# A two-layer decode kernel: reciprocal roots, weight loads and the turn's projection regrouped

## The chip, the cores and the metric

The kernel runs on one NeuronCore of a Trainium2 chip. Its engines are TensorE (PE; its weight loads are shown apart as PEld), VectorE (DVE), ScalarE (ACT), GpSimd (POOL) and SyncE (SP, which issues the DMAs). The metric is device time of one execution in microseconds (us), the median of several runs.

## What is computed

Eight sequences (B = 8) of one token each go twice through an attention layer over a cache and an MLP, with the same weights and the same cache both times. All tensors are bf16.

```python
def _A_ref(x, k_cache, v_cache, wq, wo):      # x: 8 x 1 x 448; caches: 8 x 8 x 4096 x 256
    q = (x @ wq).reshape(B, Sq, 16, 256)...   # 16 query heads on 8 kv heads
    scores = einsum("bhqd,bhkd->bhqk", q, k) * 256 ** -0.5
    o = einsum("bhqk,bhkd->bhqd", softmax(scores), v)
    return o.reshape(B, Sq, 4096) @ wo
def _B_ref(x, w1, w2, w3, w4):
    ...
    x1 = x + hs                               # with one token, hs is 0 and x1 is x
    return x1 + _gelu(_layernorm(x1) @ w3) @ w4

x = x + _A_ref(_layernorm(x), ...)
x = x + _B_ref(_layernorm(x), ...)
x = x + _A_ref(_layernorm(x), ...)
x = x + _B_ref(_layernorm(x), ...)
```

In the mixer, each quarter of the hidden state is shifted by one or two tokens; with a single token only padding is left, so w1 and w2 are not read.

## The kernel before

**Data.** K and V of one kv head are 2 MB each and come in four chunks of 512 KB. SBUF holds 31 slots of one chunk each. One DMA brings one, two or four chunks (1 MB: two). A pair `m` (0 to 3) is two kv heads of one sequence; `s` (0, 1) is the head within the pair, `c` the chunk. Names in the order of the work: A3m2 is layer 0, sequence 3, pair 2; B3m2 is the same in layer 1.

**Work on a pair.** `kpart` (L836) turns each K chunk so that TensorE can multiply it by q: by 32 x 32 block transposes on DVE (L914) into another slot, or by TensorE transposes (L832) that ACT copies back (L892). Then come the scores (L902, L923, L951) and the softmax. `vpart` (L1034) multiplies the probabilities by V in one of two ways. The usual one has the probabilities stationary and V moving (L1089), eight rows of a PSUM bank that ACT and DVE evict (L1100, L1102) and eight small matmuls gather (L1111). The other one, `still`, has V stationary (L1063); each chunk c of each head s has four columns of its own in one bank of psV, and after both heads DVE adds the four chunks (L1066, `rd`) and scales by the reciprocal sum (L1069, `o`). `still` is taken for the last pair of a sequence in layer 0 (pair 3) and for the last pair of all (sequence 7, layer 1, pair 0). `outproj` (L1130) and, for all eight sequences at once in layer 1, `outproj8` (L1143) multiply a pair's output by its rows of wo, 16 matmuls for each head (L1138, L1151), into columns of psT.

**The turn.** When layer 0 of sequence b is through, `turn(b)` (L649) takes it to layer 1. It is one chain of small instructions: add the eight partial products of wo and x (L657, L659); normalise (`norm1`, L556: column sum on PE L526, L561 to L567 on DVE, a sum over the partitions on POOL L570, a reciprocal root on DVE, `root`, L530); w3 (`project`, L582, L584); gelu (L592 to L597); w4 (`down`, L607); the residual (L668); a second `norm1`; wq for one row (`rows_`, L678, 32 matmuls, in eight groups of four, two rows of psT at each of four partition offsets; row r = 0 for heads 0 to 7, r = 1 for 8 to 15); ACT scales all of it by the root (L685); four matmuls turn it into columns (L690); and the query of pairs 1, 2 and 3 is spread for the scores (`diagonal`, L616: L630 on DVE, L637 on PE, L643 on DVE). Only then can the scores of layer 1 begin.

**What is kept.** The K of pairs 1 to 3 stays in SBUF from layer 0 to layer 1. Four of pair 3's chunks wait, transposed, in PSUM banks during the turn (`staying`, L818: two banks psK; psX and one psS; one psV and the other psS), since their slots are needed. `unpark` (L1186, L1190) copies them into slots on ACT after the turn. The piece in psS that is copied first (`unpark(b, 1, ready, [1])`, L684) is ordered after the last operation of the turn's second root.

**The root.** `root` computes 1/sqrt by a bit trick (a shift and a subtraction) and a polynomial, as eight DVE operations for one column, ten where the weight differs by column. The turn needs two of them after its first `norm1` (one for each of two norms whose sums are shared) and one after the second; the start needs one, the end two.

**Order.** Every instruction is recorded by `add` with an engine, a cost, the buffers that it reads and writes, the PSUM banks and units (loads) that it touches, and a priority. A bank may be used by one engine at a time: an operation of another engine depends on all operations of the engine before it in that bank, whatever the columns. `schedule` (L168) then fixes the order on every engine once and for all, by a list schedule that takes the lowest priority number among what is ready by its own costs. The turn's operations have -1.0, except the eight groups of wq, which have `at[0] + 1.5`, behind the V matmuls around them. Engines run their list in order and wait on semaphores. SP issues all loads in one fixed order (`order`, L1248; the stream of L1216 to L1245), each after the last readers of the slots that it overwrites. At the start that order is the rows of x, the first K pair, wq in three pieces of 128 rows and two of 64 rows (`wqt0`, `wqt1`, the last 64 rows of wq folded into the two halves of the partitions), then K, V and wo; w3 (again three pieces and two of 64 rows) and w4 come just before the V of the first sequence's pair 3.

**The end.** `end` (L768) does, for all eight sequences together, what the turn does up to the residual: add the eight partial products of psT (L777) and x (L779), normalise (`norm8`, L719), w3, two roots, gelu, w4, the residual, a transpose back (L797), a copy (L802) and the output DMA (L803).

Of the kernel before, what the change touches and what calls it, by code (L numbers as in the profile page):

```python
# [3 lines left out]
P = 128  # L4
B = 8
D = 448
HQ = 16
HKV = 8
# [3 lines left out]
NCH = 4  # L12
NSLOT = 31
SMALL = 218
# [3 lines left out]
NS = 2  # L18
# [22 lines left out]
ROOT_MAGIC = 0x5F1FFFF9  # L41
ROOT_K = 0.703952253
ROOT_C = 2.38924456
# [29 lines left out]
class Unit:  # L73


    def __init__(self, name, emit, nbytes, slotted=True):
        self.name, self.emit, self.nbytes, self.slotted = name, emit, nbytes, slotted
        self.wide = None
        self.slot = self.sem = self.val = None
        self.op = None  # L80
        self.readers = []
        self.land = None
        self.evs = [None, None]
        self.raw, self.source = False, None
        self.group, self.lead, self.pair = [self], None, None
# [273 lines left out]
def bass_interleave_layers__gqa_block_cached__mixer_s_mlp__decode_kernel(  # L359
# [49 lines left out]
    sf, rcs, stat = pack(f32, [8, NP * 4, NS * 10])  # L409
# [20 lines left out]
    def rows(u, t, ap, nbytes):  # L430
# [84 lines left out]

    ROOT = -0.375 * ROOT_K ** 5
    EPS1 = LN_EPS * D ** 3
    EPS2 = LN_EPS * LN_EPS * D ** 3 / (1.0 + LN_EPS)
    SCALE1 = -ROOT * float(D) ** 0.5
    SCALE2 = -ROOT * (D / (1.0 + LN_EPS)) ** 0.5  # L520

# [8 lines left out]
    def root(out, v, second, square, bufs, units, name, scalar=False):  # L530


        c, io = 160, i32
        eps, scale = (EPS2, SCALE2) if second else (EPS1, SCALE1)

        def op(emit, n):
            dve(emit, c, bufs if n != "0" else square, bufs, units=units, name=name + n)

        def weigh(n):

            if scalar:
                op(lambda e: e.scalar_tensor_tensor(v(2), out(), v(1), out(), ALU.mult, ALU.mult), n)
            else:
                op(lambda e: e.tensor_tensor(v(2), out(), out(), ALU.mult), n)
                op(lambda e: e.tensor_tensor(v(2), v(2), v(1), ALU.mult), n + "b")

        op(lambda e: e.tensor_scalar(v(1), v(0), eps, scale ** -2.0, ALU.add, ALU.mult), "0")
        op(lambda e: e.tensor_single_scalar(out().bitcast(io), v(1).bitcast(io), 1, ALU.arith_shift_right), "1")
        op(lambda e: e.tensor_scalar(out().bitcast(io), out().bitcast(io), -1, ROOT_MAGIC, ALU.mult, ALU.add), "2")
        weigh("3")  # L550
        op(lambda e: e.scalar_tensor_tensor(out(), v(2), -ROOT_C, out(), ALU.add, ALU.mult), "4")
        weigh("5")
        op(lambda e: e.scalar_tensor_tensor(v(2), v(2), -10.0 / (3.0 * ROOT_K ** 2), v(2), ALU.add, ALU.mult), "6")
        op(lambda e: e.scalar_tensor_tensor(out(), v(2), 5.0 / ROOT_K ** 4, out(), ALU.add, ALU.mult), "7")

    def norm1(x, bx, bx4, out0, name):  # L556


        c = 160
# [7 lines left out]
        dve(lambda e: e.tensor_tensor_reduce(out=sjk[:, :], in0=sxc[:, 0:4], in1=sxc[:, 0:4], scale=1.0, scalar=0.0,  # L567
# [4 lines left out]
        root(lambda: sf[:, 2:3], lambda k: sf[:, (1, 3, 4)[k]:(2, 4, 5)[k]], name.endswith("a"), [Bs["sq"]], [Bs["f"]], [], name + "n", True)  # L572
# [41 lines left out]
    Bo1, Bo2 = [[Buf() for _ in range(HKV // 2)] for _ in range(2)], [Buf() for _ in range(HKV // 2)]  # L614
# [34 lines left out]
    def turn(b):  # L649
# [5 lines left out]
        dve(lambda e: e.memset(sx1[64:128, 4:5], 0.0), 125, [], [Bs["x4"]], name=n + "c1")  # L655
        plan.turn = True
# [735 lines left out]
```

## Time and profile before

| what | value |
|---|---|
| median of 3 runs | 1097.46 us (1096.98 to 1097.98) |
| the profiled execution | 1098.74 us |
| its span on the core | 1095.7 us |
| mean granted TensorE clock | 0.619 |
| PE, PEld busy | 756.3 us (69%), 526.6 us (48%) |
| DVE busy | 832.6 us (76%) |
| ACT, POOL busy | 207.8 us (19%), 71.4 us (7%) |
| DMA queue of SP | 446.80 MB, 98.4% of 16 engines' span |
| L914, DVE transposes of K | x544, 649.4 us busy |
| L1089, V matmuls | x1528, 181.1 us busy |

The span is what the trace shows; 3.0 us of the execution lie around it. A timeline row gives start, duration, engine, line, operation, out<-in, shapes and count, and in brackets the idle time before it and what ended it. A row of stretches gives from:to, length, busy time of each engine with its number of instructions, the granted clock, the share of the DMA engines that is busy, and GB/s. Turn 3, used in what follows, runs from about 488.8 us (last V matmul of layer 0) to 504.2 us (first score of layer 1).

### The profile page before, as it was taken

The page shows a single profiled execution, that of the slowest core. Times are in us where ns is not written, and L with a number is a line of the kernel's source. Part 1 is how long each engine was busy: PE and PEld are TensorE (multiplying, and loading weights), DVE is VectorE, ACT ScalarE, POOL GpSimd, SP SyncE. Part 2 cuts the span into 40 slices and gives each one's busy share as a digit, 9 for nine tenths or more (in the row PEclk, how much of TensorE's full clock was granted, in tenths as well). Part 3 has the DMA queues.
Part 4 walks back from the last instruction along what each step waited for, and adds up shares of the span by engine and source line. Part 5 has one row for each costly group of instructions (what it writes and reads, how often), then busy time and mean ns, then how long its engine had stood idle before and what let it go on. Part 6 is the DMA issues. An engine that isn't in the chain of part 4 may idle for free.

```text
span 1095.7 us, 33703 instructions
## 1 busy us (share of the span) xinstructions
PE 756.3 (69%) x15400; PEld 526.6 (48%) x15400; DVE 832.6 (76%) x1595; ACT 207.8 (19%) x314; POOL 71.4 (7%) x232
## 2 busy tenths in 40 slices
PE   2566586778577865867767787577666786676864
PEld 2355454465346543555436554355444654356533
DVE  4999459964997499955899469984799739995572
ACT  1032121112021211203112032121221121121210
POOL 0000000000000000000000000000100000000000
PEclk9997566556655665556655556555655566555665
DMA  9999999999999999999999999999999999999994
GB/s 353 406 419 420 395 406 426 422 412 408 429 423 415 412 425 427 421 405 409 424 426 420 411 412 429 426 417 394 427 427 423 419 399 428 427 422 411 410 427 176
DMA packets 54846, 448.94 MB, mean 410 GB/s; under 512 B 5536, under 2 KB 11568, under 8 KB 14128
## 3 DMA queue, kind: packets, MB, share of 16 engines
q1 hardware_dynamic: 54704, 446.80, 98.4%
q8 instruction: 120, 1.97, 0.7%
q14 instruction: 22, 0.18, 0.0%
HBM read 446.77 MB, written 0.01 MB: 408 GB/s over the span
## 4 chain that ended last, share of the span: by engine, by line
DVE 39%; DMA 24%; PE 21%; issue 9%; ACT 3%; POOL 0%; POOLq 0%; DVEq 0%
DVE slots L914 29%; DMA slots<-in_A_k_cache_dram 16%; DMA slots<-in_A_v_cache_dram 8%; PE psV L1089 6%; PE psS L923 5%; DVE pT L1021 2%; PE psT L678 2%; ACT slots L892 2%; PE psS L902 2%; DVE slots L1102 1%; PE psV L1063 1%; PE psT L607 1%; PE psK L832 1%; PE psT L1138 1%; DVE qe L643 1%
## 5 line engine op out<-in xcount | busy, mean ns | idle before, releaser
L914 DVE STREAM_TRANSPOSE slots<-slots 128x1024 bf16<-128x1024 bf16 x544 | 649.4, 1228 | 33.0 <-DMA slots<-in_A_k_cache_dram 24.3
L923 PE MATMUL psS<-qe,slots 128*128 128x8 bf16 x5760 | 225.3, 175 | 152.6 <-DVE slots L914 111.5
L923 PEld LDWEIGHTS psS<-qe,slots 128*128 128x128 bf16 x5760 | 191.1, 104 | 238.5 <-DVE slots L914 176.0
L1089 PE MATMUL psV<-slots,pT 128*8 128x512 bf16 x1528 | 181.1, 550 | 17.5 <-DMA slots<-in_A_v_cache_dram 9.5
L892 ACT COPY slots<-psK 128x1024 bf16<-128x1024 bf16 x80 | 78.8, 1014 | 168.0 <-PE psK L832 167.6
L832 PE MATMUL psK<-ident,slots 128*128 128x128 bf16 x640 | 74.2, 301 | 4.2 <-DMA slots<-in_A_k_cache_dram 4.1
L1100 ACT ACTIVATE slots<-psV 128x512 bf16<-128x512 f32 x48 | 29.0, 605 | 218.5 <-PE psV L1089 218.4
L985 POOL PARTITION_ALL_REDUCE small<-small x64 | 23.8, 372 | 693.5 <-DVE small L983 582.4
L832 PEld LDWEIGHTS psK<-ident,slots 128*128 128x128 bf16 x640 | 61.1, 138 | 7.0 <-DMA slots<-in_A_k_cache_dram 4.9
L1063 PE MATMUL psV<-pT,slots 128*128 128x2 bf16 x1568 | 50.9, 166 | 17.1 <-DMA slots<-in_A_v_cache_dram 15.9
L951 PE MATMUL psS<-slots,qe 128*8 128x512 bf16 x184 | 55.4, 587 | 6.7 <-DVE slots L914 5.4
L1063 PEld LDWEIGHTS psV<-pT,slots 128*128 128x128 bf16 x1568 | 47.3, 104 | 19.7 <-DMA slots<-in_A_v_cache_dram 16.1
L1089 PEld LDWEIGHTS psV<-slots,pT 128*8 128x8 bf16 x1528 | 31.5, 90 | 50.5 <-issue 20.9
L1021 DVE STREAM_TRANSPOSE pT<-psS 128x128 bf16<-128x128 bf16 x64 | 44.9, 702 | 6.5 <-PE psS L1013 4.7
L1006 ACT ACTIVATE pT<-psS 128x128 bf16<-128x128 f32 x56 | 15.5, 277 | 178.7 <-DVE psS L1003 178.6
L1066 DVE TENSOR_REDUCE small<-psV 128x8 f32<-128x32 f32 x16 | 2.8, 174 | 58.5 <-PE psV L1063 58.5
L1111 PE MATMUL psV<-same,slots 128*128 128x4 bf16 x320 | 14.0, 166 | 43.0 <-DVE slots L1102 36.9
L630 DVE TENSOR_TENSOR qe<-psT,small 128x32 bf16<-128x32 f32 x32 | 6.1, 190 | 48.2 <-PE psS L923 34.3
L902 PE MATMUL psS<-qo,slots 128*128 128x2 bf16 x768 | 27.8, 167 | 17.6 <-ACT slots L892 10.5
L1102 DVE TENSOR_TENSOR slots<-psV,slots 128x512 bf16<-128x512 f32 x48 | 32.3, 672 | 10.0 <-ACT slots L1100 10.0
L902 PEld LDWEIGHTS psS<-qo,slots 128*128 128x128 bf16 x768 | 24.0, 101 | 25.4 <-ACT slots L892 17.1
L1111 PEld LDWEIGHTS psV<-same,slots 128*128 128x128 bf16 x320 | 11.8, 102 | 49.2 <-issue 40.8
(170 smaller groups left out, 805.8 us busy)
## 6 DMA issues: line engine op xcount, KB each, us to landing
slots<-in_A_v_cache_dram SPq DMA_DIRECT2D x149, 1024.0 KB, 9.7
slots<-in_A_v_cache_dram SPq DMA_DIRECT2D x50, 2048.0 KB, 19.1
slots<-in_A_k_cache_dram SPq DMA_DIRECT2D x44, 2048.0 KB, 18.1
slots<-in_A_k_cache_dram SPq DMA_DIRECT2D x71, 1024.0 KB, 13.7
slots<-in_A_v_cache_dram SPq DMA_DIRECT2D x14, 512.0 KB, 8.1
wo_sb<-in_A_wo_dram SPq DMA_DIRECT2D x4, 896.0 KB, 19.5
wq_sb<-in_A_wq_dram SPq DMA_DIRECT2D x3, 1024.0 KB, 9.1
w_sb<-in_B_w_dram SPq DMA_DIRECT2D x1, 1568.0 KB, 16.9
```

The lines of the kernel that those rows point to most:

```text
L832: last = e.transpose(tile[:, j * P:(j + 1) * P], slots[u.slot][:, o:o + P], ident[:, :])
L892: return e.copy(slots[u.slot][:, 1024 * t:1024 * t + 1024], tile)
L902: last = e.matmul(o, slots[u.slot][:, i:i + P], q, start=(cc == 0), stop=(cc == 1))
L914: return e.transpose(o, i)
L923: last = e.matmul(o, slots[u.slot][:, i:i + P], qe[:, 128 * k + 64 * s + 8 * g:128 * k + 64 * s + 8 * g + 8], start=(g == 0), stop=(g == 7))
L951: last = e.matmul(o, q, K[:, lo:hi + 1:hi - lo, :, g, :], start=(g == 0), stop=(g == 7))
L1021: add("dve", lambda e: e.transpose(pZ[:, :, 0:3:2].rearrange("p n s r -> p n r s"), psS[x][:, 128:192].bitcast(bf).rearrange("p (n r s) -> ...
L1063: last = e.matmul(o, slots[u.slot][:, i:i + P], w, start=(j == 0), stop=(j == 7))
L1089: last = e.matmul(psV[x][32 * i:32 * i + 8, :].rearrange("p (k d) -> p k d", k=2), w, v, start=(s == 0 and c == 0), stop=(s == 1 and c == ...
L1100: add("act", lambda e: e.activation(part(0), psV[x][:, :], ACT.Copy), 590, [], [Bhalf[0]], [bV[x]], [v], prio=at - 1, name=n + "ve0").targ ...
L1102: add("dve", lambda e: e.tensor_tensor(part(1), psV[x][:, :], part(0), ALU.subtract), 590, [Bhalf[0]], [Bhalf[1]], [bV[x]], [v], prio=at - ...
L1111: last = e.matmul(to[:, 4 * cc:4 * cc + 4].rearrange("p (s h) -> p s h", s=2), part(k // 2)[:, i:i + P], w, start=(k == 0), stop=(k == 3))
```

## The change

Six edits:

1. **Root**: another bit trick (one multiplication of the bit pattern by -1/2) and other polynomials: six operations for one column, eight where the weight differs. For the turn's roots the scale and epsilon are put into the sum of squares (`scale`, `scalar` of L567), and the other norm's root takes one operation more, seven in all.
2. **`still`**: all four chunks of a head add up in PSUM (four columns for a head), with no `rd`; each head is scaled by itself as soon as its four chunks are done (`o0`, `o1`). In layer 1 the two heads have different psV banks, in layer 0 the same one.
3. **Output projection of the last pair, by head**: its 16 matmuls for head 0 are issued after `o0`, those of head 1 after `o1`. The turn and the end add up the earlier products and x beforehand (`ao`, `xa`), then the first head's product (`xb`), and at last the second one's (`x1`).
4. **Turn's wq in two halves**: heads 0 to 7 into psT as before, heads 8 to 15 into the psS bank whose parked piece is copied out first; one row each; each is scaled by ACT into its own half of a slot (`qr0`, `qr1`) and turned into columns by itself (`qc0`, `qc1`). The groups have the turn's priority, -1.0. The first copy out of psS is ordered after the third of the root's six operations (`plan.ops[-4]`).
5. **Loads**: the four 64-row pieces of wq and w3 come first of all; `wqt1` and `w3t1` are issued by ACT ahead of everything else that it does, the other two by SP ahead of x.
6. `small` is two columns wider; a root's scratch has one part more.

The order that results on PE around turn 3 (V: L1089 or L1063 in the old line numbers, W: one head's 16 matmuls of the output projection, aS and bS: the column sums L526, wq00 to wq13: the groups of L678, ve: an eviction):

```
before: A3m3 V00 V01 V02 V03 V10 V11 V12 V13, B2m2V00, W30 W31, B2m2V01, aS, w3, V02 V03, w4, V10, bS, V11,
        wq00 wq01, V12 V13, wq02 wq03 wq10 wq11 wq12 wq13, B2m3V00 V01, qc, V02, q1s, V03, scores
after:  A3m3 V00 V01 V02 V03, W30, V10 V11 V12 V13, W31, B2m2V00, aS, V01, w3, V02 V03, w4, V10, bS, V11,
        wq00 wq01 wq02 wq03, V12 V13, wq10 wq11, qc0, wq12 wq13, B2m3V00, q1s, V01, qc1, scores (V02, V03 among them)
```

and on ACT: before, eviction of B2m2, copy out of psS, `qr`; after, copy out of psS, `qr0`, eviction of B2m2, `qr1`.

The diff, cut to its core:

```diff
-ROOT_MAGIC = 0x5F1FFFF9
+ROOT_MAGIC = 0x5F3759DF - 2 ** 31
...
+    U_side = [U_wq.pop()]
...
+    U_side.append(U_w3.pop())
+    for u in U_side:
+        u.side = True
+    U_even = [U_wq.pop(), U_w3.pop()]
+    wq_rest, w3_rest = ([U_side[i], U_even[i]] for i in range(2))
...
+        if first:
+            op(lambda e: e.tensor_scalar(v(1), v(0), *first), "0", True)
+        op(lambda e: e.tensor_scalar(out().bitcast(io), v(1).bitcast(io), -0.5, ROOT_MAGIC, ALU.mult, ALU.add), "1")
+        if scalar:
+            op(lambda e: e.scalar_tensor_tensor(v(2), out(), v(1), out(), ALU.mult, ALU.mult), "2")
+        else:
+            op(lambda e: e.tensor_tensor(v(2), out(), out(), ALU.mult), "2")
+            op(lambda e: e.tensor_tensor(v(2), v(2), v(1), ALU.mult), "2b")
+        op(lambda e: e.scalar_tensor_tensor(v(3), v(2), ROOT_Q[0], v(2), ALU.add, ALU.mult), "3")
+        op(lambda e: e.scalar_tensor_tensor(v(2), v(2), ROOT_P[0], v(2), ALU.add, ALU.mult), "4")
+        op(lambda e: e.scalar_tensor_tensor(out(), v(3), ROOT_Q[1], out(), ALU.add, ALU.mult), "5")
+        op(lambda e: e.scalar_tensor_tensor(out(), v(2), ROOT_P[1], out(), ALU.add, ALU.mult), "6")
...
-        dve(lambda e: e.tensor_reduce(sjk[:, :], psT[:, 0:32].rearrange("p (s c) -> p c s", c=4), axis=AX.X, op=ALU.add),
+        dve(lambda e: e.tensor_reduce(sjk[:, :], psT[:, 0:24].rearrange("p (s c) -> p c s", c=4), axis=AX.X, op=ALU.add),
             180, [], [Bs["jk"]], [bT], name=n + "ao")
-        dve(lambda e: e.tensor_tensor(sx1[:, 0:4], sjk[:, :], x[:, 0:4], ALU.add), 150, [Bs["jk"], Bx[b]], [Bs["x1"]], name=n + "x1")
+        dve(lambda e: e.tensor_tensor(sjk[:, :], sjk[:, :], x[:, 0:4], ALU.add), 150, [Bs["jk"], Bx[b]], [Bs["jk"]], name=n + "xa")
+        outproj(*last, [0])
+        dve(lambda e: e.tensor_tensor(sjk[:, :], psT[:, 24:28], sjk[:, :], ALU.add), 150, [Bs["jk"]], [Bs["jk"]], [bT], name=n + "xb")
+        outproj(*last, [1])
+        dve(lambda e: e.tensor_tensor(sx1[:, 0:4], psT[:, 28:32], sjk[:, :], ALU.add), 150, [Bs["jk"]], [Bs["x1"]], [bT], name=n + "x1")
...
-        ready = plan.ops[-1]
+        ready = plan.ops[-4]
...
+        v, bank = kept[b, 3][1, 0], staying(b, 1)[1]
+        E = unpark(b, 1, ready, [1], -1.0)
+        Brow, B2 = [Buf(), Buf()], [(psT, bT), (psS[parts[0, b, 2].x], bank[1])]
         for r in range(2):
+            to, bb = B2[r]
...
-                        last = e.matmul(psT[32 * g:32 * g + 2, :], syn[:, 4 - r if k == 3 else k, 1 - r:3 - r], w,
-                                        start=(r == 0 and k == 0), stop=(r == 1 and k == 3))
+                        last = e.matmul(to[32 * g:32 * g + 1, :], syn[:, 4 - r if k == 3 else k, 1:2], w, start=(k == 0), stop=(k == 3))
...
+            R = add("act", lambda e, to=to, part=part: e.activation(part(), to[:, :], ACT.Copy, scale=sf[:, 2:3]), 590,
+                    [Bs["f"]], [Brow[r]], [bb], [v], name=n + f"qr{r}")
+            R.deps[E] = False
...
+        columns(0)
+        diagonals[1, b, 1] = diagonal(1, b, 1)
+        C = columns(1)
...
-            x = bank
             for s in range(2):
+                x = bank ^ s if layer else bank
...
-                            o = psV[x][:, 16 * s + 4 * c + 2 * cc:16 * s + 4 * c + 2 * cc + 2]
+                            o = psV[x][:, 4 * s + 2 * cc:4 * s + 2 * cc + 2]
...
-            add("dve", lambda e: e.tensor_reduce(red.rearrange("p (s k) -> p s k", s=2),
+                made.append(add("dve", lambda e, s=s, x=x: e.tensor_tensor(both(out_)[:, s], psV[x][:, 4 * s:4 * s + 4].rearrange("p (c j) -> p c j", c=2),
+                                                                           rc[:, s].unsqueeze(1).to_broadcast([P, 2, 2]), ALU.mult),
+                                110, [Brc[y]], [bo[s]], [bV[x]], prio=at - 1, name=f"{n}o{s}"))
...
-    order = [U_s0] + stream[:1] + U_wq + stream[1:10] + U_wo + stream[10:]
+    order = U_side[:1] + U_even[:1] + U_side[1:] + U_even[1:] + [U_s0] + stream[:1] + U_wq + stream[1:10] + U_wo + stream[10:]
...
+        if e == "act":
+            for u in U_side:
+                u.emit(eng, u).then_inc(u.sem, 16)
```

The end is changed like the turn: `eao` adds six of the eight parts, `exa` x, `exb` the first head's and `ex1` the second head's product of the last pair.

More of the change, by code (lines that the diff above doesn't have):

```diff
@@ L528, in total, with root @@
         add("pe", emit, 110, bufs + [Bwgt], [], [bT], units, name=name)
[L530 removed]
+    def root(out, v, first, square, bufs, units, name, scalar=False):
         c, io = 160, i32
[L534 to L554, printed above, removed]
@@ new lines, in turn, with columns, emit @@
+            R.deps[E] = False
+        def columns(r):
+            def emit(e):
+                for j in range(4):
+                    last = e.matmul(psT[:, 64 + 16 * r:80 + 16 * r].rearrange("p (g j) -> p j g", j=4)[:, j],
+                                    slots[v.slot][:, 512 * r + P * j:512 * r + P * j + P],
+                                    ident[:, :].rearrange("p (g r) -> p r g", g=4)[:, 0], start=True, stop=True)
+                return last
+            return add("pe", emit, 300, [Brow[r], Bc], [], [bT], [v], name=n + f"qc{r}", n=4)
@@ L1205, in V @@
             ahead.append((b, m, s, -0.5 if s == HKV // 2 - 1 else at[0] + 1.5))
-            for x in [x for x in ahead if x[0] <= turns[0]]:
+            for x in [x for x in ahead if x[0] <= turns[0] and x[2] < HKV // 2 - 1]:
                 outproj(*x)
```

115 lines of the change are left out of this document (59 added, 56 removed).

## The prediction

> **What bounds the kernel now.** I read the page's DMA rows first, then stretches of the trace around one turn, then the timelines of that turn and of the end.
>
> ```profile
> DMA  9999999999999999999999999999999999999994
> GB/s 353 406 419 420 395 406 426 422 412 408 429 423 415 412 425 427 421 405 409 424 426 420 411 412 429 426 417 394 427 427 423 419 399 428 427 422 411 410 427 176
> ...
> HBM read 446.77 MB, written 0.01 MB: 408 GB/s over the span
> ```
>
> The DMA engines are busy in every slice, at about 422 GB/s where nothing disturbs them, while DVE, the busiest compute engine, has 76%. 446.77 MB at 422 GB/s are 1058.7 us of the 1095.7. So the time is this stream, and the other 37.0 us are the start, dips of the rate and the end. An edit pays only where it fills one of these.
>
> Stretches of turn 3 (us; granted clock, DMA share, GB/s):
>
> ```profile
> 480.55:490.55 10.00, 0.50 0.99 383
> 490.55:498.55 8.00, 0.50 1.02 422
> 498.55:504.55 6.00, 0.82 0.92 345
> 504.55:514.55 10.00, 0.65 1.01 424
> ```
>
> Two dips: (422-383)/422 x 10 = 0.92 us just before the turn's chain and (422-345)/422 x 6 = 1.09 us at its end. The same cuts at all eight turns lose 0.1, 0.4, 0.6, 0.9, 0.6, 0.7, 0.4, 0.5 (4.2 us) and 0.8, 0.8, 0.5, 1.1, 0.7, 1.0, 0.9, 0.7 (6.5 us). **10.7 us is all that the turns can give**, however long their chains of small instructions are.
>
> Why the second dip? PE rows of the timeline:
>
> ```profile
> 495.55 1.65 PE L607 MATMUL psT<-qe,w_sb 128*128 128x1 bf16 x56 [0.91 <-DVE qe L597]
> 497.13 0.60 PE L1089 MATMUL psV<-slots,pT 128*8 128x512 bf16 x4
> 497.67 0.26 PE L526 MATMUL psT<-small 128*128 128x1 bf16 x4
> 497.86 0.60 PE L1089 MATMUL psV<-slots,pT 128*8 128x512 bf16 x4
> 498.47 1.02 PE L678 MATMUL psT<-wq_sb,qe 128*2 128x512 bf16 x8
> 499.28 1.07 PE L1089 MATMUL psV<-slots,pT 128*8 128x512 bf16 x8
> ```
>
> In a turn only four pairs of slots rotate; SP reissues a pair when L1089 (or L1063) has consumed it. The V pair that landed at 495.8 is consumed only at 498.46, since PE's fixed order puts it behind the MLP's down product (L607) and the column sum (L526), which waits on the chain. SP's issues stand at 491.31, 494.68, 498.50, 500.39: 3.4 and 3.8 us apart where 1 MB takes 2.48 us at 422 GB/s. Their times to landing fall from 9.3 us to 8.4 and 7.1: the queue ran dry. So the links of the turn count only as far as they release PE for the V matmuls.
>
> **The end**, from the last V piece on (PE and DVE rows):
>
> ```profile
> 1082.28 1.01 PE L1063 MATMUL psV<-pT,slots 128*128 128x2 bf16 x32 [1.63 <-DMA slots<-in_A_v_cache_dram]
> 1083.33 0.19 DVE L1066 TENSOR_REDUCE small<-psV 128x8 f32<-128x32 f32 x1 [7.14 <-PE psV L1063]
> 1083.55 0.19 DVE L1069 TENSOR_TENSOR qo<-small 128x8 bf16<-128x8 f32 x1
> ...
> 1083.80 1.02 PE L1151 MATMUL psT<-qo,wo_sb 128*128 128x8 bf16 x32 [0.51 <-DVE qo L1069]
> 1084.86 0.42 DVE L777 TENSOR_REDUCE slots<-psT 128x32 f32<-128x256 f32 x1 [1.11 <-PE psT L1151]
> 1085.31 0.19 DVE L779 TENSOR_TENSOR slots<-slots,small 128x32 bf16<-128x32 f32 x1
> ```
>
> After the last V piece nothing runs beside this chain, so each link taken out is time. The start, in stretches (busy times of PE, PEld, DVE, ACT, POOL, then clock, DMA share, GB/s):
>
> ```profile
> 2.00:4.00 2.00, 0.00 (x0) 0.00 (x0) 1.65 (x6) 0.01 (x1) 0.00 (x0) 1.00 0.80 229
> ...
> 13.00:14.00 1.00, 0.80 (x11) 0.80 (x12) 0.90 (x7) 0.00 (x0) 0.00 (x0) 1.00 0.99 193
> 14.00:15.00 1.00, 1.00 (x12) 0.93 (x9) 0.45 (x3) 0.62 (x1) 0.00 (x0) 1.00 1.07 254
> 15.00:16.00 1.00, 0.19 (x2) 0.00 (x0) 0.00 (x0) 1.00 (x2) 0.00 (x0) 1.00 1.06 238
> ```
>
> The stream ramps up until 4 us (0.47 MB moved: 2.9 us lost) and then drops to about 230 GB/s where the two 64-row pieces of wq pass; with the stretch 16 to 17 (377) that is 1.5 us lost.
>
> **The change, part by part.**
>
> *End.* The sum over the chunks moves into PSUM, so L1066 and its gap go: 1083.33 to 1083.55, 0.22. Only the second head's 16 matmuls of L1151 follow the last piece: half of 1.02, 0.51. The wide L777 is done ahead of it, and one addition of L779's price stays: 1084.86 to 1085.31, 0.45. Together 1.18. The two reciprocal roots go from 10 to 8 operations each; the 20 of before run interleaved from 1087.41 (L547) to 1089.43 (L743), 2.02 us, so 4 of them are 0.40. The up product beside them ends near 1088.0, before their new end, so it doesn't catch up. **-1.6 us** (-1.2 if a semaphore hop eats the gaps, -1.8).
>
> *Start.* wq's and w3's 64-row pieces (0.75 MB) go first, one half of each from SP, the other from ACT, whose table load (0.73, 1.28 us) moves behind two issues of some 0.4 us (SP's first: 0.39); ACT's next work is at 14.38, so that is free. The 1.5 us of the slow stretch and 0.2 us at 116 to 120 (0.11 MB of w3 tail twice at 306) vanish there; K's first load is issued two issues later (1.18 to about 2.0), and the small loads must fill the ramp. SP's first big load goes out 0.44 earlier (0.74 for 1.18). If the halves run side by side: -0.44 - 1.7 = -2.1. If they keep 230 GB/s: 0.75 MB take 3.3 us where 422 takes 1.8, so 1.5 comes back, less what the ramp hides: -0.6 to -2.1. No row of before has ACT issuing or two queues at once: I take **-1.4**, nearer to the case with the ramp, as 2.9 us of it are empty. Upper end +0.4: two issues of 0.4 ahead of K that hide nothing. The stream never waits for q here (422 from 17 on), so the shift goes through to the end.
>
> The Trainium skill, "DMA: Bandwidth & Descriptors", section "Rules for kernel authors", speaks against this part: two transfers to disjoint partition halves serialize, because both spray over the same 16 engines, and issuing from several engines saves only issue time. By that rule the halves would keep their slow rate. The rows at 13 to 16 are of one queue and can't decide.
>
> *Turns.* Chain: a head's output is scaled alone, so between the last V matmul (488.81) and x1 there remain one scaling (0.18), 16 matmuls (0.50) and one addition (0.17) with hops: x1 ends near 489.8, not 491.17. A V block (0.6) now stands ahead of the column sum L526 instead of ahead of the projection, so 1.1 of these 1.3 us are left. First roots: 13 operations where 16 took 1.7 us, -0.3. The down product then starts near 494.1 (495.55) and ends before the V pair lands at 495.8; that pair is consumed by 497.3 (498.46), with L526 still between its halves, and SP's issue comes 1.1 us earlier. What that is worth I read from the other loads of the turns, by how far an issue is ahead of the moment at which the packets of the load before it begin: at 0 (this load) the stream lost 0.4 to 0.8 us, at 0.7 to 0.95 0.3 to 0.45, at 1.0 to 1.4 0.2 to 0.4, at 1.7 0.2. So **-0.35 per turn**.
>
> Against it: (1) Both heads still share a psV bank in layer 0, and the scaling of head 0 reads it, so the first V matmul of head 1 now waits for V03, the scaling (0.18) and, in PE's order, for 16 matmuls of the output projection (0.50): with hops 0.9 us. It ran at 485.52 right behind. Behind it on PE stand only the last two V pieces, which land at 487.76, but SP's next issue (486.57) waits for it and goes out near 487.5, in the first dip: from 1.7 us ahead to 0.8, +0.25 per turn. (2) The wq products now outrank the V pair that landed at 498.1: all of the first half (16, two groups of 1.02) stand ahead, 497.3 to 499.3; the pair (1.07) is done at 500.4, as before (500.36): 0. (3) The second half waits for the parked piece of psS (ACT L1190, 1.01), now started after the third of six root operations: 498.6 to 499.6, ahead of the pair's end (500.4), so nothing behind it on PE is later: 0. Scores of the turn start near 502.7 instead of 504.16; that releases loads which lie 5 to 8 us behind the packets, so it is hidden. Net -0.1 x 8, and I take **-1.0** with rounding; ends -6.5 (the whole second dip) and +5.5 (below).
>
> **Sum**: -1.6 - 1.4 - 1.0 = **-4.0**. The profiled execution has 1098.74 (span 1095.70 and 3.04 around it), so 1094.7 for such a one; it lies 1.28 above the median of the runs, 1097.46, which gives **1093.5**.
>
> **Rivals.** *Links in full*: if the V pair's issue is early enough, the second dips (6.5 us) go: -1.6 - 1.4 - 6.5, 1088.0. For it: the chain is 1.6 to 2 us shorter; against: V11 stays behind L526. 0.12. *Half rate stays*: the 64-row pieces run at 230 GB/s from two queues as from one, and the ramp hides none of it, -0.6 for the start: 1094.3. For it, the rows at 13 to 16; against it, the empty ramp. 0.20. (This is where the skill's rule would lead.) *Only the end counts*: the stream's dips merely move and the start is filled with the same slow bytes: 1095.9, no measurable change (the runs spread over 1.0 us, and 0.2%, 2.2 us, is about what can be told). 0.14. *Slower*: head 1's V wait, (1). If scaling and projection hold it 1.7 us or more instead of 0.9, the issue falls behind the packets and the full dip of 0.84 comes, +0.7 x 8 = 5.5, against -1.6 - 1.4: 1100.0. It needs V03 late or a busy DVE; DVE is idle from 483.3 to 488.85. 0.06. The forecast keeps 0.48.
>
> Faster 0.80, same 0.14, slower 0.06. The range: down to 1089.0, where the end and the start are at their lower bounds (-0.9) and the turns give two thirds of the second dips (-4.6 for -1.0); up to 1096.5, the third rival and 0.6 for the spread of the runs. It leaves out the first and the last rival, 0.18.
>
> **What would show it.** End: from the last V matmul's end to the output's issue 9.2 us instead of 10.75. Start: no stretch under 300 GB/s at 13 to 16, full rate by 4.5. Turns: dip at the chain's end about 0.5 us instead of 0.8, the one before it larger by 0.2; V11 of the pair done 1.1 us earlier. Wrong, if the dips vanish altogether, or if the first 5 us lose more than 4.

## The result and the profile after

| | median (runs) | range | ratio to before, 95% interval |
|---|---|---|---|
| before | 1098.04 us (14) | 1096.98 to 1100.22 | |
| changed | 1096.53 us (14) | 1093.48 to 1099.53 | 0.9984 [0.9976, 0.9991] |
| changed, a second series | 1095.28 us (12) | 1093.99 to 1098.15 | 0.9975 [0.9964, 0.9986] |

The change saves 1.5 us in the first comparison and 2.8 us in the second; all its 26 runs together have a mean of 1096.13 us with a standard error of 0.31, and before has 1098.36 (0.09) over the 157 runs that were made of it. That is 2.2 us with an error of 0.3; 4.0 were forecast. Part of the distance to 1093.5 is the starting point: three runs had given a median of 1097.46 for before, later series gave 1097.9 to 1098.4.

The profiled execution has 1096.3 us, its span 1094.5. The page's row of GB/s looks like that of before:

```profile
GB/s 357 405 420 417 411 400 428 422 404 409 428 422 417 411 428 426 422 395 423 426 426 419 399 423 426 426 416 398 427 428 424 400 406 426 426 423 414 416 425 188
...
HBM read 446.77 MB, written 0.01 MB: 408 GB/s over the span
```

The stream is still the bound, so again the dips have to be looked at. The stretches of turn 3, with the cuts of before moved by the 0.4 us by which the last V matmul of layer 0 ends earlier (488.42; after the length come the busy times of PE, PEld, DVE, ACT and POOL with their instructions, then clock, DMA share, GB/s):

```profile
480.15:490.15 10.00, 7.60 (x201) 6.41 (x198) 3.09 (x15) 0.28 (x1) 1.21 (x4) 0.50 0.98 367
490.15:498.15 8.00, 7.40 (x152) 4.14 (x152) 4.34 (x33) 0.40 (x2) 0.80 (x2) 0.50 1.00 413
498.15:504.15 6.00, 4.70 (x90) 2.11 (x83) 1.97 (x8) 3.60 (x5) 0.00 (x0) 0.95 1.01 421
504.15:514.15 10.00, 9.73 (x277) 7.51 (x277) 4.47 (x12) 4.53 (x6) 0.94 (x3) 0.57 1.01 420
```

The second dip (345 GB/s before) is gone: 421. The first one is deeper, 367 for 383. That is the main reading of this case, and the chain's PE rows show why the second one went:

```profile
493.73 1.66 PE L609 MATMUL psT<-qe,w_sb 128*128 128x1 bf16 x56 [0.33 <-DVE qe L599]
495.31 0.60 PE L1115 MATMUL psV<-slots,pT 128*8 128x512 bf16 x4
495.85 0.26 PE L531 MATMUL psT<-small 128*128 128x1 bf16 x4
496.04 0.60 PE L1115 MATMUL psV<-slots,pT 128*8 128x512 bf16 x4
496.65 1.45 PE L695 MATMUL psT<-wq_sb,qe 128*1 128x512 bf16 x12
...
498.31 0.83 PE L1115 MATMUL psV<-slots,pT 128*8 128x512 bf16 x8
```

The down product starts 1.82 us earlier (493.73 for 495.55), and the V pair that waited for it is through at 496.65 instead of 498.46. The next rows are the price in front of it, head 1's first V matmul (x16 at 486.13) behind the projection of head 0:

```profile
485.68 0.59 PE L1163 MATMUL psT<-small,wo_sb 128*128 128x1 bf16 x16 [0.33 <-DVE small L1096]
486.13 0.56 PE L1089 MATMUL psV<-pN,slots 128*128 128x2 bf16 x16
486.55 0.56 PE L1089 MATMUL psV<-pT,slots 128*128 128x2 bf16 x16
```

The end, PE and then DVE:

```profile
1082.51 1.01 PE L1089 MATMUL psV<-pT,slots 128*128 128x2 bf16 x32 [1.44 <-DMA slots<-in_A_v_cache_dram]
1083.79 0.59 PE L1178 MATMUL psT<-qo,wo_sb 128*128 128x8 bf16 x16 [0.27 <-DVE qo L1096]
```

```profile
1083.55 0.18 DVE L1096 TENSOR_TENSOR qo<-psV,small 128x4 bf16<-128x4 f32 x1 [3.77 <-PE psV L1089]
1084.49 0.19 DVE L803 TENSOR_TENSOR slots<-psT,slots 128x32 bf16<-128x32 f32 x1 [0.75 <-PE psT L1178]
```

One scaling, 16 matmuls and one addition are left of the links. From the last V matmul's end (1083.52) to the output's issue (1092.82) it is 9.30 us; before 10.75. The start:

```profile
2.00:4.00 2.00, 0.00 (x0) 0.00 (x0) 1.65 (x6) 1.25 (x1) 0.00 (x0) 1.00 0.87 231
4.00:6.50 2.50, 0.00 (x0) 0.00 (x0) 0.09 (x2) 0.00 (x0) 0.00 (x0) 1.00 1.04 228
13.00:14.00 1.00, 1.00 (x12) 1.00 (x11) 0.93 (x5) 0.45 (x1) 0.00 (x0) 1.00 1.06 442
14.00:15.00 1.00, 0.37 (x4) 0.10 (x1) 0.84 (x1) 1.00 (x2) 0.00 (x0) 1.00 1.01 418
15.00:16.00 1.00, 0.00 (x0) 0.00 (x0) 0.00 (x0) 0.48 (x1) 0.00 (x0) 1.00 0.96 385
```

The slow stretch has moved from 13 to 16 us to 4 to 6.5 us, where the ramp of before was over (423 GB/s). From two queues the 64-row pieces run at 228 GB/s, as from one (193 to 254). This is what the Trainium skill says in "DMA: Bandwidth & Descriptors", section "Rules for kernel authors": halves of the partitions serialize, and a second issuing engine gives no bandwidth. The trace agrees in the rate, and the DMA share is 1.04 there, so the 16 engines were busy with them.

So at the start little is won: counted against 422 GB/s, the first 20 us lose 4.3 us (4.0 in the second series) for 4.6 in before. More is won where w3 passes, from 116 to 120 us; before, then changed:

```profile
116.00:120.00 4.00, 2.58 (x88) 2.43 (x89) 4.00 (x7) 0.00 (x0) 0.00 (x0) 0.80 1.07 306
116.00:120.00 4.00, 1.50 (x44) 1.36 (x45) 4.00 (x7) 0.00 (x0) 0.00 (x0) 0.50 1.05 379
```

From 104 to 128 us, where w3 and w4 pass, before loses 1.7 us and the changed kernel 0.6. With w3's 64-row pieces among them, the packets of the other weight loads took longer too (means from 110 to 122 us: 158 ns for 143 with 3584 bytes, 46 for 41 with 896 bytes).

### The profile page after: what moved, and what is told of

It reads as the page before. It is cut to its first block, busy times and chain, and to the rows that moved or that the text cites. A ratio compares the mean times of both kernels' runs of the same rounds, so it can differ in the third digit from the quotient of the medians.

```text
span 1094.5 us, 33709 instructions
## 1 busy us (share of the span) xinstructions
PE 764.3 (70%) x15416; PEld 525.1 (48%) x15416; DVE 830.5 (76%) x1567; ACT 212.2 (19%) x322; POOL 72.0 (7%) x232
## 4 chain that ended last, share of the span: by engine, by line
DVE 39%; DMA 26%; PE 20%; issue 7%; ACT 3%; POOL 1%; SPq 0%; DVEq 0%; POOLq 0%
DVE slots L938 31%; DMA slots<-in_A_k_cache_dram 17%; DMA slots<-in_A_v_cache_dram 9%; PE psV L1115 5%; PE psS L947 4%; DVE pT L1045 2%; PE psS L926 2%; PE psV L1089 2%; PE psT L609 1%; ACT slots L916 1%; DVE slots L1128 1%; PE psT L695 1%; PE psT L1163 1%; PE psK L856 1%; ACT slots L1217 1%
## 5 line engine op out<-in xcount | busy, mean ns | idle before, releaser
L1115 PE MATMUL psV<-slots,pT 128*8 128x512 bf16 x1528 | 183.7, 555 | 20.0 <-DMA slots<-in_A_v_cache_dram 15.2
L1089 PE MATMUL psV<-pT,slots 128*128 128x2 bf16 x1568 | 50.6, 165 | 9.6 <-DMA slots<-in_A_v_cache_dram 9.0
L1089 PEld LDWEIGHTS psV<-pT,slots 128*128 128x128 bf16 x1568 | 47.2, 104 | 11.6 <-DMA slots<-in_A_v_cache_dram 9.1
L1163 PE MATMUL psT<-small,wo_sb 128*128 128x1 bf16 x1024 | 35.7, 166 | 7.1 <-DVE small L1096 4.7
L926 PE MATMUL psS<-qo,slots 128*128 128x2 bf16 x768 | 28.0, 167 | 13.4 <-ACT slots L916 10.4
L1163 PEld LDWEIGHTS psT<-small,wo_sb 128*128 128x128 bf16 x1024 | 32.5, 105 | 9.2 <-DVE small L1096 6.0
L1137 PEld LDWEIGHTS psV<-same,slots 128*128 128x128 bf16 x320 | 11.8, 103 | 49.6 <-issue 42.3
L1096 DVE TENSOR_TENSOR small<-psV,small 128x4 bf16<-128x4 f32 x30 | 4.3, 144 | 41.1 <-PE psV L1089 41.1
## 6 DMA issues: line engine op xcount, KB each, us to landing
slots<-in_A_k_cache_dram SPq DMA_DIRECT2D x69, 1024.0 KB, 14.3
```

The costliest lines, as they stand in the source:

```text
L926: last = e.matmul(o, slots[u.slot][:, i:i + P], q, start=(cc == 0), stop=(cc == 1))
L1089: last = e.matmul(o, slots[u.slot][:, i:i + P], w, start=(c == 0 and cc == 0 and j == 0), stop=(c == NCH - 1 and cc == 1 and j == 7))
L1115: last = e.matmul(psV[x][32 * i:32 * i + 8, :].rearrange("p (k d) -> p k d", k=2), w, v, start=(s == 0 and c == 0), stop=(s == 1 and c == ...
L1163: last = e.matmul(psT[:, 4 * (2 * s + i) + c:4 * (2 * s + i) + c + 1], wo_sb[:, a, d0:d0 + P], o1[b % 2][:, a:a + 1], start=(k == 0), stop ...
```

## The experiments

The measure of the dips in what follows: the time of a stretch minus its bytes divided by 422 GB/s, summed over the eight turns, with the stretches laid from the end of the last V matmul of layer 0 (0). One profiled execution gives it to about 1 us only: two executions of one kernel differ by 1.3 (changed) and 1.5 (both parts undone) in the sum.

| kernel | median (runs) | ratio to before [95%] | -24 to -4 | -4 to +3 | +3 to +30 | sum |
|---|---|---|---|---|---|---|
| before | 1098.04 (14) | | 3.4 | 3.4 | 7.7 | 14.5 |
| changed | 1096.53 (14) | 0.9984 [0.9976, 0.9991] | 6.0 | 5.2 | 2.8 | 14.0 |
| the same again | 1095.28 (12) | 0.9975 [0.9964, 0.9986] | 6.1 | 6.7 | 2.6 | 15.3 |
| e1 heads undone | 1095.27 (7) | 0.9975 [0.9964, 0.9985] | 3.3 | 3.6 | 8.0 | 14.9 |
| e2 W behind | 1096.17 (11) | 0.9980 [0.9971, 0.9988] | 6.4 | 5.4 | 4.4 | 16.2 |
| e3 loads undone | 1097.41 (11) | 0.9987 [0.9979, 0.9996] | 6.9 | 6.4 | 3.3 | 16.6 |
| e4 roots and end alone | 1096.77 (12) | 0.9988 [0.9980, 0.9997] | 4.8 | 4.0 | 5.7 | 14.5 |
| f3 heads and halves undone | 1095.29 (10) | 0.9975 [0.9966, 0.9985] | 2.9 | 5.0 | 4.6 | 12.5 |
| the same again | 1095.53 (12) | 0.9976 [0.9966, 0.9986] | 2.9 | 4.8 | 6.3 | 14.0 |
| f2 one scaling | 1096.04 (11) | 0.9981 [0.9973, 0.9990] | 2.5 | 4.3 | 9.5 | 16.4 |
| g1 heads without halves | 1097.37 (12) | 0.9991 [0.9979, 1.0003] | 6.1 | 5.8 | 2.3 | 14.3 |
| h1 last pair only | 1094.53 (6) | 0.9965 [0.9953, 0.9977] | 4.2 | 5.9 | 2.0 | 12.1 |
| h3 earlier pair only | 1098.10 (12) | 0.9993 [0.9983, 1.0003] | 6.0 | 5.0 | 6.5 | 17.5 |

**Undoing one part at a time.** The heads of layer 0 (edits 2 and 3 there, in every pair of layer 0 that takes `still`; the rest is the changed kernel):

```diff
-        if still:
+        if still and layer == 0:
...
+        elif still:
...
-        outproj(*last, [0])
...
-        outproj(*last, [1])
+        outproj(*last)
```

> The changed kernel with one part undone: in layer 0 the last pair again has a sum over chunks and one scaling for both heads, and its output projection follows whole; the rest (roots, wq halves, loads, end) stays changed. Lost stream time is counted against 422 GB/s, over the eight turns, in stretches that start from the end of the last V matmul of layer 0: -10 to -4, -4 to +3, +3 to +9, +9 to +16 us. Before: 0.9, 3.4, 0.7, 6.6 (11.6 in all); changed: 2.9, 5.2, 1.5, 1.1 (10.7). Theory A (the first head's eviction and projection, which the second head's first V matmul now waits for, cost the dip in front of the turn): the first two stretches return to about 1 and 3.5, and the last one to 2 to 4, since the chain is 1.1 us longer again; in all 8 to 9, the time 1.5 to 2.5 us below the changed kernel, so 0.35% below the one before. Theory B (four pairs of slots rotate, and what they lack appears in one place or another): 10.5 to 11.5 in all, the time within 1 us of the changed kernel.

1095.27 us: not slower than the changed kernel. Whatever the heads bring at the second dip (8.0 without them, 2.8 with them) is lost elsewhere. A second series gave 1095.46 (11 runs; 6.3 at the second dip, 13.4 in all):

> The kernel with layer 0's heads undone once more, beside the others on this chip: 1095.3 us again (0.9975 of before) if the 1.3 us between it and the changed kernel are real, about 1096.3 if they were chance.

The wait that I had priced at +0.25 a turn is partly the output projection of head 0, so it was put behind the pair's last V matmul:

```diff
         outproj(*last, [0])
+        plan.ops[-1].deps[next(o for o in plan.ops if o.name == f"A{b}m3V11")] = False
```

> The changed kernel with the first head's 16 projection matmuls ordered behind the second head's second V piece, so that the second head's first V matmul waits only for the scaling (0.2 us with its hop) and no longer for 0.5 us of TensorE. Theory A: -4 to +3 loses about 4.0 over the eight turns instead of 5.2, the other stretches stay, the time is 1 us lower than the changed kernel's. Theory B: what is won there comes back at +9 to +16, in all 10.7 as before, and the time stays within 0.5 us.

1096.17 us, 0.2 us below the changed kernel by the means with an error of 0.5, and the stretch from -4 to +3 stays at 5.4 where theory A had 4.0. So this half of the wait isn't it. The loads in the old order, from SP alone:

```diff
-    U_side = [U_wq.pop()]
+    U_side = []
...
-    order = U_side[:1] + U_even[:1] + U_side[1:] + U_even[1:] + [U_s0] + stream[:1] + U_wq + stream[1:10] + U_wo + stream[10:]
+    order = [U_s0] + stream[:1] + U_wq + stream[1:10] + U_wo + stream[10:]
```

> The changed kernel with the loads' order as before (64-row pieces in their old places, all issued by SP). Theory A (the halves stay at about 230 GB/s from two queues, and the ramp hides almost nothing): the first 20 us lose 4.6 instead of 4.3, and the stretch of w3 and w4 0.3 to 0.8 more; the time is 0.3 to 1.0 us above the changed kernel. The theory of the prediction (the ramp hides them): 1.4 us above. Theory C (ACT's two issues or the second queue disturb something later): below the changed kernel.

1097.41 us, 0.9 us more than the first series of the changed kernel (1.0 by the means, error 0.5), the size of theory A, though the error does not exclude 1.4. The first 20 us lose 5.0 us, and the stretch from 104 to 128 us loses 1.7, both more than theory A had. And before with nothing but the new roots and the end by heads (edits 1 and 6, and 2 and 3 in layer 1):

> The kernel before with only the new roots and the end by heads: layer 0's heads, the turn's wq and the loads are all as before. Both theories: from the last V matmul's end to the output's issue 9.3 instead of 10.75 us, so at least 1.4 us below the kernel before. Theory A: the turn's second dip shrinks by a little (chain 0.7 us shorter by the roots: 6.6 to about 5), nothing grows in front of the turn, 2 to 3 us below the kernel before, so at or below the changed one. Theory B: exactly the end, 1.4 us below.

1096.77 us. With the new loads added to that kernel (which is the changed one with heads and halves undone):

> The kernel before with the new roots, the new loads and the end by heads, but with layer 0's heads and the turn's projection as before: it differs from the kernel with the heads undone by the halves of the projection alone. If these halves bring what the sums of the runs so far leave for them (0.6 to 1.1 us), 1096.0 to 1096.4 us; if they bring nothing, 1095.3 us.

1095.29 us. So roots and end give 1.2 us and the loads 1.4 to 1.6 more, each by the medians against before, measured beside it (1097.99; 1097.88 and, in a second series, 1098.34). The traces show where the loads give it: from 104 to 128 us the three kernels with the old loads (before, e3, e4) lose 1.7 to 1.8 us and every kernel with the new ones that still loads w3 0.6 to 0.7; in the first 20 us it is 4.6 to 5.0 against 3.9 to 4.5. So about 1.1 us come from w3's stretch and about 0.5 from the start. The halves of the projection give nothing beside heads as before: with them 1095.27 and 1095.46, without them 1095.29 and 1095.53.

**What sets the dips?** Two theories: the length of the turn's chain, or the rotation of the few free pairs of slots. The first kernel leaves out the MLP of the turns:

```diff
-        norm1(sx1[:, :], Bs["x1"], Bs["x4"], 40, n + "a")
...
-        dve(lambda e: e.scalar_tensor_tensor(x[:, 0:4], psT[:, 32:36], 0.5, sxy[:, :], ALU.mult, ALU.add), 150,
-            [Bs["xy"]], [Bx[b]], [bT], name=n + "r2")
+        dve(lambda e: e.tensor_copy(x[:, 0:4], sx1[:, 0:4]), 150, [Bs["x1"]], [Bx[b]], name=n + "r2")
```

> The changed kernel whose turns leave out the inner MLP (x1 is copied to x; w3 and w4 are still loaded, and the last layer still uses them), so that a turn's projection starts about 4.5 us earlier after the last V matmul, with the same 31 slots and the same transfers. Stream time lost from 10 us before to 16 us after the last layer-0 V matmul, summed over eight turns, is 10.7 us in the changed kernel. Chain theory (the shortage is the wait of the V pair's and K's scores for the turn's chain): it falls below 3 us and the run takes 1086 to 1089 us. Rotation theory (four pairs of slots turn round in front of the turn, each held from its load's issue to its last reader, and the shortage lies wherever that rotation is cut, so that it moves and does not vanish): the sum stays at 9 to 12.5 us and the run at 1094.5 to 1097 us.

1093.06 us (5 runs; 0.9952 [0.9940, 0.9964]). From the last V matmul to the projection it is 2.3 us instead of 8.5, 6.2 us less and more than I had written; 8 x 6.2 = 50 us of chain bring 3.5 us against the first series of the changed kernel. The dips lose 11.8 us as against 14.0. So the chain's length alone is not what the dips are, though the time lies below the rotation theory's window too. Then the same chain made longer, behind the residual:

```diff
+        for i in range(8):
+            dve(lambda e: e.tensor_copy(x[:, 0:4], x[:, 0:4]), 150, [Bx[b]], [Bx[b]], name=n + f"r{i}")
```

> The changed kernel with eight copies of x onto itself between the MLP's end and the second normalization, 0.15 us each by the rows of such copies: every turn's chain is 1.2 us longer, all else the same. Chain theory: 8 x 1.2 = 9.6 us more, 1105 to 1107 us. Rotation theory: little of it comes out, 1096 to 1099 us, the sum over the turns 10 to 13 us.

1100.07 us (12 runs; 1.0012 [0.9999, 1.0024]), 3.5 us more for 8 x 1.7 us of chain (10.2 us to the projection for 8.5): between the theories. A shorter chain is worth 7% of itself, a longer one 26%. One slot less (`NSLOT = 30`):

> The changed kernel with 30 slots instead of 31; nothing else is edited, and the planner makes its order anew. A slot is 0.5 MB, 1.24 us of the stream at 422 GB/s. Chain theory: each turn's wait begins 1.24 us of stream earlier, 8 x 1.24 = 10 us more, all of it behind the turn's start. Rotation theory: at least as much more, but lost in front of the turn's start as well as behind it, and a pair less where pairs are needed: 1106 to 1118 us.

1105.09 us (6 runs; 1.0065 [1.0052, 1.0077]), 8.6 us more, the most of it behind the turn's start (13.7 us from +3 to +30). And four slots more, in the room of w3 and w4, with the MLP left out in the turns and at the end:

> The changed kernel without the MLP in the turns and at the end, without the transfers of w3 and w4 (3.2 MB, 7.6 us at 422 GB/s), and with 35 slots in the room that they leave. Chain theory: the same sum over the turns as in the kernel without the turns' MLP, as its chain is the same. Rotation theory: two more pairs turn round, so that the sum over the turns falls from about 11 us to under 3 us; with the transfers and the end's MLP gone the run is at 1073 to 1078 us by it, and at 1081 to 1086 us if the sum stays.

1075.64 us (4 runs), in the window of the rotation theory, but the loss from -10 to +16 is 8.3 us, not under 3: about 1 us per turn stays with whatever chain and however many slots. Neither theory holds alone. In these runs the kernel stands at a bend: one slot less or later releases cost, earlier ones bring little.

**Where the heads cost.** Two kernels take head 0's scaling out of head 1's way: the second head in the other bank (`x = bank ^ s` in both layers),

> The changed kernel with the second head of a layer-0 pair accumulated in the other psV bank, as layer 1 does it, so that its first V matmul needs no scaling of head 0; the piece parked in that bank is transposed after it. Lag theory (what the heads' part costs is the first head-1 pair of slots, released 2.2 us after its landing instead of 1.3, because its V matmul stands behind head 0's scaling and 16 output-projection matmuls): the lag falls to about 1.7, as the projection still stands ahead of it on PE, the stream time lost from 4 us before to 3 us after the last V matmul falls from 5.2 to about 4.3 us over eight turns, and the run takes about 1095.8 us. If the heads' part costs something else (the order that the planner makes of everything after it), 1096.5 us as in the changed kernel, or more.

and one scaling for both heads after the last V matmul in layer 0:

> The changed kernel in which layer 0 scales both heads with one operation after the last V matmul; the sums stay in PSUM. Nothing stands between the V matmuls of the two heads any more, both halves of the output projection follow the scaling, so that x1 comes about 0.5 us later. Lag theory: the lag of the first head-1 pair falls from 2.2 to 1.1 to 1.3 us, the loss from -4 to +3 us falls from 5.2 to about 3.6 us, and the run takes 1095.3 us as with the heads undone. Otherwise 1096.5 us or more.

The first has 1097.99 us (11 runs) where 1095.8 were expected: the piece parked in that bank now comes later, and the pair behind the last V matmul goes out at +4.6 to +5.2 us instead of +2.1 to +2.6 in turns 1 to 7. The second has 1096.04 us (11 runs); head 1's first pair is released 1.3 us after its landing for 2.2, as expected, but the second dip is back (9.5 us from +3 to +30). So neither is a better kernel, and a wait of head 1 was still only a suspect. Two more kernels take it apart, the heads without the halves, and the wait without the heads:

> The changed kernel with the turn's projection in one piece as before: it differs from the kernel with heads and halves undone (1095.3 us) by layer 0's heads alone. If the heads cost about 1 us, 1096.1 to 1096.6 us; if that cost comes only with the halves, 1095.3 us; by my forecast of the turns, 1094.3 us.

1097.37 us (12 runs; 0.9991 [0.9979, 1.0003]): some 2 us slower than the kernel without either. Beside the new heads the halves do bring something, then: 1.5 us by the means (1097.62 to 1096.13, error 0.5).

```diff
+                for k in range(4 * (1 - s)):
+                    add("dve", lambda e: e.tensor_copy(red[:, 0:4], psV[x][:, 0:4]), 150, [], Bred, [bV[x]], prio=at - 1, name=f"{n}d{k}")
```

> The kernel with heads and halves undone, in which four small DVE copies read the sums of head 0 before the first V matmul of head 1 may write their bank (four of 0.15 us and hops, about 0.8 us in all; the copies' results are used nowhere, and PE's order is the same). The wait of the changed kernel is there, and nothing that it is paid for. If the late release of that pair costs what the first dip shows (0.2 to 0.25 us per turn), 1097.0 us, 1.6 to 2 us more than without; if the rotation takes it up, 1095.3 to 1095.8 us.

Its PE and DVE rows show that the wait is there, 0.84 us ahead of head 1's first V matmul:

```profile
485.07 0.58 PE L1077 MATMUL psV<-pN,slots 128*128 128x2 bf16 x16 [0.84 <-DVE small L1081]
```

```profile
484.26 0.75 DVE L1081 COPY small<-psV 128x4 f32<-128x4 f32 x4 [2.39 <-PE psV L1077]
```

1095.58 us (12 runs; 0.9979 [0.9970, 0.9989]), by the means 0.2 us above the kernel without it, with an error of 0.4: the rotation takes the wait up. Beside it, the changed kernel:

> The changed kernel again, on this chip: 1096.5 us if what has been measured of it holds.

It came out 1.2 us lower than that, so two series of one kernel can differ by as much as some of the parts that are compared here. What remains is a place, and DVE's groups name it; of before, then of the changed kernel:

```profile
L1066 DVE TENSOR_REDUCE small<-psV 128x8 f32<-128x32 f32 x16 | 2.8, 174 | 58.5 <-PE psV L1063 58.5
```

```profile
L1096 DVE TENSOR_TENSOR small<-psV,small 128x4 bf16<-128x4 f32 x30 | 4.3, 144 | 41.1 <-PE psV L1089 41.1
```

A last pair per sequence and one at the end would be 9 reductions, not 16, and 16 scalings in layer 0, not 30. The loop that issues the stream takes `still` for the pair *before* the last as well (pair 2 of sequences 1 to 7), which neither my description of the kernel above nor the forecast noticed; seven pairs are scaled and projected by heads there, 8 to 20 us ahead of the last V matmul. (The kernel with the wait has it in these pairs too, so this wait is not their cost either.) Separating the two pairs, first one scaling for both heads in all but the last pair (for the other half of the cut, `m == 3`):

```diff
+                if layer == 0 and m != 3:
+                    continue
...
+            if layer == 0 and m != 3:
+                made.append(add("dve", lambda e, x=x: e.tensor_tensor(both(out_), psV[x][:, 0:8].rearrange("p (s c j) -> p s c j", s=2, c=2),
...
```

> The changed kernel in which layer 0 scales head by head only in a sequence's last pair of heads; the pairs before it have one scaling for both heads, behind their last V matmul, and their output projection behind that. If the heads' cost lies with the earlier pairs, the loss from 24 to 4 us ahead of the last V matmul falls from 6.0 to about 3 us, and the run takes 1094.0 to 1095.3 us, the forecast's turns at last; if it lies with the last pair, 1095.7 to 1096.5 us.

1094.53 us (6 runs), in the window of the earlier pairs and the fastest of those that leave nothing out, 3.8 us below the kernel before beside it (1098.34). The loss from -24 to -4 falls to 4.2 us only, not to 3. The kernel with both parts undone, again:

> The kernel with heads and halves undone again, on this chip: 1095.2 us.

1095.53 us. And the other half of the cut:

> The changed kernel in which the last pair of a sequence has one scaling for both heads, and the pair before it is scaled head by head: the other half of the cut of the run before. If the cost lies in the earlier pair, the stream still loses about 6 us from 24 to 4 us ahead of the last V matmul, and the run takes 1096.5 to 1097.3 us; if not, 3 us there and 1095.5 us.

1098.10 us, more than expected, with 6.0 us lost from -24 to -4 as expected. Together with the kernel with one scaling in both pairs (f2) this makes four kernels that differ only in which of the two pairs is scaled and projected by heads (means; the error of a difference is 0.5 to 0.6):

| | last pair: one scaling | last pair: by heads |
|---|---|---|
| earlier pair: one scaling | 1096.17 (f2) | 1094.82 (h1) |
| earlier pair: by heads | 1097.80 (h3) | 1096.13 (changed) |

By heads, the earlier pair costs 1.6 and 1.3 us, and the last pair brings 1.4 and 1.7 us. Counted from before as measured beside each series, it is 1.2 and 1.5, and 1.8 and 1.5. So the two cancel in the changed kernel. Against the kernel with heads and halves undone (1095.52), h1 has 0.7 us less (error 0.5); that is what the last pair and the halves bring over the old form, if they bring it.

What differs there in the order of PE can be seen at turn 4; first the changed kernel, then the one with both parts undone:

```profile
600.99 0.38 PE L947 MATMUL psS<-qe,slots 128*128 128x8 bf16 x8 [0.74 <-DVE small L1096]
601.23 0.56 PE L1163 MATMUL psT<-small,wo_sb 128*128 128x1 bf16 x16
601.65 1.01 PE L856 MATMUL psX<-ident,slots 128*128 128x128 bf16 x8
```

```profile
600.22 0.38 PE L936 MATMUL psS<-qe,slots 128*128 128x8 bf16 x8 [0.75 <-DVE slots L927]
601.03 1.04 PE L845 MATMUL psX<-ident,slots 128*128 128x128 bf16 x8 [0.44 <-DMA slots<-in_A_k_cache_dram]
```

Head 0's projection of the earlier pair (x16) now stands right ahead of the transposes of the last K pieces, which otherwise start when their data lands. In the fixed order of PE it does so in sequences 1 to 7 of every kernel with the heads in that pair and 31 slots, 16 to 20 us ahead of the last V matmul; in f2, h1 and the kernels with both parts undone both heads' matmuls stand behind those transposes, 8 to 10 us ahead of it. But three kernels that have it there (two banks, no MLP, longer chain) lose only about 3 us from -24 to -4. So the pair is shown by the four kernels; that it is this block, and not the later V matmuls or the scaling between DVE's transposes, was not tried by itself.

## Why the prediction was wrong

- **End, -1.6: right.** 10.75 to 9.30 us is -1.45. The same 9.2 to 9.4 us stand in every profiled variant that has the new roots, the end by heads and 31 slots, whatever the rest of it does. In time roots and end alone gave 1.2.
- **Start, -1.4: the size came out, in good part by luck.** The loads gave 1.4 to 1.6 us by the medians without heads and halves, 0.9 with them. But the 64-row pieces kept their slow rate, and the ramp hid almost none of it (3.0 us lost in the first 4 us, as before): the start itself gave about 0.5 us, which is the -0.6 of the rival *half rate stays*. The other 1.1 us came from w3's stretch, priced at 0.2. That price counted the two 64-row pieces alone; the whole 4 us at 306 GB/s lose 1.1 us by the row that it was taken from. "Full rate by 4.5" was wrong (228 GB/s up to 6.5), no stretch under 300 GB/s at 13 to 16 right.
- **Turns, -1.0: this step failed.** Without heads and halves the kernel stands at -2.6 to -2.8 us, which is the end and the loads. With them 1.0 more was to come, and it stands 0.6 us higher instead (1096.13 for 1095.52; the error of 0.4 leaves open whether it is a loss, but not that the gain is missing). The term priced what heads and halves do in the last pair of a sequence, and put their effect on the pair before it at nothing, since it was not seen that this pair takes `still` too. There they cost 1.2 to 1.6 us. The "x16" in the group of L1066 would have told it.
- In the last pair the step was near: -0.7 (error 0.5) with that pair alone, -1.0 forecast, of which -0.2 was rounding. The parts were further off. The second dip gave 4.9 us of 7.7, not 2.8; the first one took 1.8 (3.2 in the second execution) for 2.0; and in time the late V matmul of head 1, my +0.25 a turn, costs 0.2 us in all (error 0.4).
- *Only the end counts* (1095.9) came nearest in time and was wrong in kind: the loads were worth 1.4 us, and the dips moved in part.
- The turns cannot be summed dip by dip, either. Over before, changed, heads undone and both undone the second dip lies between 2.6 and 8.0 us and the sum stays at 12.5 to 15.3 us.

## What to carry to other kernels

When a branch of a helper (a function that is used in several places) is changed, count the instances of its line in the profile before pricing one of them: the group's "x16" against the 9 expected would have shown the second user. In a stream that runs on a few rotating buffers a dip that vanishes is no gain until the dips before and behind it have been added up, in more than one execution. Where a list scheduler fixes the order, making something ready earlier also moves it ahead of work that others wait for, at every place where the code is used.

## What the runs showed of the hardware

- With 2.2 MB of issued loads not yet moved, the stream still thinned: at turn 3 of the changed kernel to 254 GB/s in the half microsecond from 480.5 us.
- The last bytes of the stream taper for about 4 us, although the last load had been issued 25 us ahead (1052.84): from 1077 us on, 401, 295, 180, 98 and 25 GB/s in the changed kernel.
- Loads of 64 rows ran at 193 to 254 GB/s from one queue and at 228 from two, with the DMA engines' share at 1.0, beside 422 for loads of 128 rows.
- The changed kernel varies more from run to run than the kernel before: a standard deviation of 1.6 us over 26 runs, for 1.1 over 157.
